# A static order planned with longer landings for two reciprocal rows and for queued transfers, with later second weights and fewer adding transfers

## The chip, the cores and the metric

The kernel runs on one core of a Trainium2 chip. Its engines run side by side, each through its own list of instructions: TensorE (PE; its weight loads are shown apart as PEld), VectorE (DVE), ScalarE (ACT), GpSimd (POOL) and SyncE (SP). ACT, POOL and SP also issue DMA transfers. The time is the device time of one execution in microseconds (us), the median of several runs.

## The reference

Four batches, 12 heads, 448 positions, head size 64; the model width is 768, the inner width 3072.

```python
scores = cap * tanh(scale * q @ k.T / cap)                 # soft cap
attn = exp(scores - max);  attn /= attn.sum(-1) + 1e-9
x = (attn @ v) laid out as [batch, seq, 768]
h = x.T @ U @ V                                            # U: 448x32, V: 32x448
u = x + h.T
out = u + relu(u @ w_ch1) @ w_ch2                          # 768 -> 3072 -> 768
```

## The kernel before

**The order.** The Python program lists some thousands of tasks. Each has its engine (or several to choose from) with a planned duration, what it reads and writes, a priority, and for a transfer a planned time to landing (`lat`) and a planned share of the DMA queues (`size`). `simulate` (from L155) plays the list once as a list scheduler: an engine that is free takes the ready task of the lowest priority number. `emit` then writes the tasks out in that order, engine by engine, with the semaphores that they need. So a planned number changes no instruction; it changes where the instructions stand. On the chip each engine keeps its order and waits where something comes later than planned. In `simulate` one clock, `moved`, stands for the DMA queues: each sized transfer pushes it on by its `size`, and the transfer counts as landed no earlier than `moved` + 500 ns.

**Attention** (to about 187 us) works on pairs of heads (p = 1 to 24). For two pairs at a time `normalize` (L591 to 632) makes the reciprocal of the softmax sums: PE sums by ones (L600), a copy, a small transfer that spreads the row over 32 partitions (L607), DVE's reciprocal (L616), a transfer to DRAM (L611, tile `rd`), two transfers that bring it back broadcast to 128 partitions (L624, tile `rb`), all three kinds issued by POOL; and DVE multiplies `u` by `rb` (L629, `norm`). `mixin` (from L634) then forms u = x + (x.T U V).T for the pair: PE transposes (L650) into two banks, two copies to `xx`, PE products with U (L666), a copy to `ys`, PE products with V (L677), and two additions on DVE (L684). The chains of the last two pairs (p of 20 and more) lie within the next stage.

**First layer, "up"** (L817; 185.5 to 509.6 us). u @ w_ch1 is formed by Strassen-Winograd with seven block products; each factor is split into a high and a low part, so that each task is nine matmuls of 128x128 by 128x448 into one PSUM bank `mm`. The batches 0 and 1 go first (n = 0, to about 350 us), then 2 and 3 (n = 1). In each there are 12 chunks of two weight blocks. A raw weight block comes as two words per value into one of two tiles `wr` (L739), is converted to `wa` (L328 on ACT, L333 and L336 on DVE), kept in DRAM (L749 for first weights, L746 for second weights, there `quad`), and made into the split operands `ws` by ACT and DVE (L717, L710). The results pass through `cx`: `keep` copies a bank to it on ACT (L272 from `up_seven`), DVE adds another bank to it (L830), and POOL stores it to DRAM as `mid` (L843). L272 is the copy helper that all stages use. The table `SECONDS` says how many blocks of w_ch2 are converted beside each chunk: entry 0 for n = 0, entry 1 for n = 1, entry 2 for the next stage.

**Second layer, "down"** (L963; 509.6 to 823 us). Three groups of inner blocks, in each the seven products of `PORDER`, each with six tasks of 12 matmuls. `weight` loads a weight quarter `wb` from `quad` (L889), `token` loads `gq` or `gw` from `mid` (L896); both are issued by SP. ACT and DVE split them into high and low parts (the weights into a tile that shows as `bw` or `wl`, the tokens into `g`; L272 and L908). Each finished bank is added to `u` by `onto`: on DVE (L983), or, every `EVERY`-th time, by an ACT copy to `st` (L272) and a POOL transfer that adds into `u` (L988). The last products of the last group send `u` out (L977).

Of the kernel before, what the change touches and what calls it, by code (L numbers as in the profile page):

```python
# [27 lines left out]
CF = 2  # L28
NCH = NF // CF
GROUPS = (0, 1), (2, 3), (4, 5)  # L30
EVERY = 3
SECONDS = (0, 0, 1, 0, 1, 0, 1, 0, 1, 0, 0, 0), (0, 0, 1, 1, 1, 1, 1, 2, 1, 2, 1, 1), (2, 2, 2, 2)
PORDER = 2, 1, 3, 6, 5, 7, 4


# [56 lines left out]
class Plan:  # L92
# [43 lines left out]
    def simulate(self):  # L136
# [11 lines left out]
        def rooms(bufs):  # L148
            taken, n, out = {}, {}, []
            for b in bufs:  # L150
                k = n.get(b.tag, 0)
                if self.order[b.tag][head[b.tag] + k] is not b:
                    return None
                n[b.tag] = k + 1
                for p in b.pools:  # L155
                    at = p, p.at(b)
                    if p.free[at[1]] > taken.get(at, 0) and all(not q.due for q in p.after):
                        taken[at] = taken.get(at, 0) + 1
                        out.append(p)
                        break  # L160
                else:
                    return None
            return out
# [14 lines left out]
        def start(t, e):  # L178
            new = [b for b in t.bufs if b.pool is None]
            for b, p in zip(new, rooms(new)):  # L180
                p.free[p.at(b)] -= 1
                b.pool = p
                b.slot = p.idle[p.at(b)].pop(0)
                head[b.tag] += 1
            cost = max(t.durs[e] - OVER.get(e, 0), 60) + (SWITCH if t.mode != mode[e] else 0)
            mode[e] = t.mode
            t.at, t.eng = now, e
            out.append(t)
            free[e] = now + cost
            if t.lock and e in locked:  # L190
                locked[e] = now + cost
            for o in t.durs:
                ready[o].remove(t)
            heapq.heappush(events, (now + cost, 1, t.i, "e"))
            done = now + cost + OVER.get(e, 0) + (LAT[e] if t.lat is None else t.lat)
            if t.size:
                self.moved = max(self.moved, now + cost + 1800) + t.size
                done = max(done, self.moved + 500)
            heapq.heappush(events, (done, 2, t.i, "d"))

        while True:
            for e in LAT:
                if free[e] <= now and ready[e]:
                    for t in sorted(ready[e], key=lambda t: (t.prio, t.i)):
                        if can(t, e):
                            start(t, e)
                            break
            if not events:
                break
            now = events[0][0]  # L210
            while events and events[0][0] == now:
                _, _, i, what = heapq.heappop(events)
                t = self.tasks[i]
# [65 lines left out]
class Build(Plan):  # L279
# [305 lines left out]
    def normalize(self, p):  # L585

        nc = self.nc
        prio = p - 100
        e = self.es[p - 1], self.es[p]
        rth, rj = self.rest[p]  # L590
        rest = p >= RESTS  # L591
        s = self.psum("misc")
        sr = self.buf("sr", [128, S], F32, self.an)
        r7 = self.buf("r7", [128, S // 32], F32, self.aq)
        u = self.u_bufs[p // NP]
        dram = {}

        def sums():
            for i in range(4):
                nc.tensor.matmul(  # L600
                    s.t[32 * i:32 * i + 32, :S], self.ones[:, 0], e[i % 2].t[:, i // 2], start=True, stop=not rest)
            for i in range(4 if rest else 0):
                nc.tensor.matmul(
                    s.t[32 * i:32 * i + 32, :S], self.ones[:, 1 + i % 2], rth.t[:, rj, i // 2], start=False, stop=True)

        def spread():
            nc.gpsimd.dma_start(out=r7.t, in_=sr.t[::32].rearrange("h (p f) -> h p f", p=32))  # L607

        def put():
            d = dram[0] = self.dp.tile([4, S], F32, tag="rd", name="rd", bufs=4)  # L610
            nc.gpsimd.dma_start(out=d.rearrange("a (p f) -> (a p) f", p=32), in_=r7.t)  # L611

        self.task({"PE": 1500 if rest else 750}, sums, r=[(e[0], 0), (e[1], 0), *([(rth, rj)] if rest else [])], w=[(s, 0)], prio=prio, mode="s")
        self.task({"DVE": 620, "ACT": 560}, lambda e: self.copy(e, sr.t, s.t[:, :S]), r=[(s, 0)], w=[(sr, 0)], prio=-300)
        self.task({"POOL": 700}, spread, r=[(sr, 0)], w=[(r7, 0)], lat=3000, prio=prio)
        self.task({"DVE": 250}, lambda: nc.vector.reciprocal(r7.t, r7.t), w=[(r7, 0)], prio=prio)  # L616
        self.task({"POOL": 600}, put, r=[(r7, 0)], w=[("rd", p)], lat=4000 if p < 20 else 2500, prio=prio)
        rb = self.buf("rb", [128, 2, S], F32, self.an)
        q = p % NP - 1

        def get():
            rows = dram[0].rearrange("(a i) s -> a (i s)", a=2)
            for a in range(2):
                nc.gpsimd.dma_start(  # L624
                    out=rb.t[64 * a:64 * a + 64].rearrange("p i s -> p (i s)"), in_=rows[a:a + 1].broadcast_to((64, 2 * S)))

        def norm():
            x = u.t[:, q:q + 2]
            nc.vector.tensor_tensor(out=x, in0=x, in1=rb.t, op=ALU.mult)  # L629

        self.task({"POOL": 1100}, get, r=[("rd", p)], w=[(rb, 0)], lat=7800 if p == 1 else 5000 if p < 20 else 3800, prio=prio)
        self.task({"DVE": 1090}, norm, r=[(rb, 0)], w=[(u, q), (u, q + 1)], prio=prio, lock=True)

    def mixin(self, b, pp):  # L634
# [139 lines left out]
    def moe(self):  # L774
# [4 lines left out]
        for n, bs in enumerate(((0, 1), (2, 3))):  # L779
            ws = None if n else self.strassen_weights(0, True, 60000, ALONE - 90, (self.wg,))  # L780
            xs = self.operands(bs, ORDER if n else EARLY, -50 if n else ALONE - 90)
            for c in range(NCH):
                prio = 3 if n or c < NCH - 2 else -60
                ws = ws or self.strassen_weights(c, n == 0, 0, prio)
                for _ in range(SECONDS[n][c]):
                    self.block(1, next(seconds), True, 0, 3)
# [94 lines left out]
    def down_all(self, order, seconds):  # L881


        nc, K, prio = self.nc, DM // 2, 3
# [26 lines left out]
        for ms in GROUPS:  # L911
            a, b, s2, w, g, bank = {}, {}, {}, {}, {}, {}
            last = ms is GROUPS[-1]
            for x, p in enumerate(PORDER):
                for _ in range(SECONDS[2][x - 3] if ms is GROUPS[0] and x > 2 else 0):
                    self.block(1, next(seconds), True, 0, prio, (self.cr,))
                for m in ms:
                    for i, j in {2: ((0, 1),), 1: ((0, 0),), 3: ((1, 0), (1, 1))}.get(p, ()):
# [13 lines left out]
                    x = w[p, m] = self.buf("wl", [128, 2, 2, K], F32R, self.bw, self.wq, self.cr)  # L932
# [18 lines left out]
                for n, bs in enumerate(((0, 1), (2, 3))):  # L951
                    u0, u1 = (self.u_bufs[i] for i in bs)
                    for d in range(3):
# [5 lines left out]
                        def products(p=p, n=n, d=d, ps=ps, fresh=fresh, w=w, g=g, ms=ms):  # L959
# [9 lines left out]
                            w=[(ps, 0)], prio=order, mode="mm")  # L969
# [3 lines left out]
                        for u, e in onto:  # L973
                            count += 1
                            self.onto(ps, lambda u=u, k=e: u.t[:, k], (u, e), count % EVERY == 0 and not (last and p in (7, 4)))
                            if last and p in (1, 5, 7, 4) and (p != 5 or e < 3):
# [69 lines left out]
```

## Time and profile before

| | |
|---|---|
| median of 3 runs | 829.42 us (828.74 to 830.03) |
| the profiled execution | 828.35 us; its span is 826.6 us, so 1.75 us lie outside the span |
| busy in the span | PE 805.9 us (97%), DVE 676.8 (82%), ACT 481.1 (58%), POOL 123.0 (15%) |
| mean granted TensorE clock | 0.993 of full speed |
| transfers | 164.28 MB, 199 GB/s on average |

The span is the time from the first to the last instruction of the profiled execution, and all stretches (such as 205.27) are counted from its start. A row of a timeline is a run of equal instructions of one engine: its start, its busy time, the engine, the line, the operation, output and input with one instruction's size, and in brackets how long the engine stood idle before it and what released it. The names of tiles stand without their numbers there. Matmuls overlap and their ends are modelled, so the distance from one start to the next is a better measure of a run than its busy time. The clock is given as a share of the full 2.4 GHz: 0.50 is the lower of the two levels, 1.2 GHz.

### The profile page before, as it was taken

The numbers are of one execution on the slowest core, as the hardware profiler recorded it, in microseconds if no ns is written. First come the engines' busy times: TensorE is split into PE (matmuls) and PEld (weight loads), VectorE is DVE, ScalarE is ACT, GpSimd is POOL, SyncE is SP. The second block draws the span as 40 slices with busy tenths as digits, with TensorE's granted clock in tenths as the row PEclk, the third lists the DMA queues.
The fourth block names the chain that finished last, engine by engine and source line by source line (L and its number), as shares of the span: only waits on it lengthen the run. The fifth ranks groups of instructions, "written<-read, shape, count | busy, mean of one in ns | idle before, by whom it ended". The sixth has DMA issues, their size and how long they took to land.

```text
span 826.6 us, 11913 instructions
## 1 busy us (share of the span) xinstructions
PE 805.9 (97%) x4344; PEld 639.0 (77%) x4344; DVE 676.8 (82%) x1067; ACT 481.1 (58%) x686; POOL 123.0 (15%) x193
## 2 busy tenths in 40 slices
PE   9999999997999999999999997999999999999998
PEld 4333333335899899989999996999999999999997
DVE  4778899988789888999786882899989987798653
ACT  7999999985565666565445543445444344433430
POOL 0111111111111111111111211011210112110110
PEclk9999999999899999999999999999999999999999
DMA  6453454526589897447866854977996477534252
GB/s 232 134 181 116 135 155 120 182 82 206 192 287 306 291 309 271 161 149 256 284 238 244 254 203 145 379 229 234 341 314 191 106 196 190 153 80 123 45 145 90
DMA packets 56109, 164.28 MB, mean 199 GB/s; under 512 B 7634, under 2 KB 22898, under 8 KB 56050
## 3 DMA queue, kind: packets, MB, share of 16 engines
q1 hardware_dynamic: 34736, 106.82, 39.4%
q0 software_dynamic: 14400, 37.82, 17.1%
q10 hardware_dynamic: 6914, 18.88, 5.8%
q8 instruction: 34, 0.56, 0.3%
q14 instruction: 25, 0.20, 0.1%
HBM read 106.81 MB, written 46.49 MB: 185 GB/s over the span
## 4 chain that ended last, share of the span: by engine, by line
PE 59%; DVE 2%; DMA 1%; issue 0%; ACT 0%; ACTq 0%
PE mm L963 37%; PE mm L817 22%; DMA wr<-in_w 1%; DVE cx L830 0%; DMA wb<-quad 0%; DVE x L717 0%; DVE wr L710 0%; ACT wa L328 0%; DVE ta L710 0%; DVE bw L908 0%; ACT bw L272 0%; DVE ws L717 0%; DVE u L983 0%; DVE wr L333 0%; DVE x L274 0%
## 5 line engine op out<-in xcount | busy, mean ns | idle before, releaser
L817 PE MATMUL mm<-x,ws 128*128 128x448 f32 x1404 | 291.3, 367 | 2.0 <-DVE cx L830 1.4
L817 PEld LDWEIGHTS mm<-x,ws 128*128 128x128 f32 x1404 | 263.6, 189 | 28.4 <-DVE cx L830 3.5
L963 PE MATMUL mm<-g,bw 128*128 128x448 f32 x756 | 176.1, 368 | 3.5 <-ACT bw L272 3.3
L963 PE MATMUL mm<-g,wl 128*128 128x448 f32 x756 | 174.0, 365 | 0.0
L963 PEld LDWEIGHTS mm<-g,bw 128*128 128x128 f32 x756 | 142.3, 188 | 16.2 <-ACT bw L272 3.6
L963 PEld LDWEIGHTS mm<-g,wl 128*128 128x128 f32 x756 | 142.6, 189 | 12.1 <-issue 0.2
L272 ACT ACTIVATE st<-mm 128x448 f32<-128x448 f32 x44 | 24.0, 546 | 142.4 <-issue 91.7
L843 POOL DMA_DIRECT2D mid<-cx x96 | 55.6, 580 | 258.2 <-ACT cx L272 252.7
L983 DVE TENSOR_TENSOR u<-u,mm 128x448 f32<-128x448 f32 x100 | 61.1, 616 | 36.6 <-PE mm L963 27.5
L272 ACT ACTIVATE cx<-mm 128x448 f32<-128x448 f32 x96 | 48.9, 543 | 61.7 <-PE mm L817 44.5
L503 PE MATMUL sc<-qk 64*128 64x448 f32 (+1 forms) x384 | 77.2, 569 | 0.3 <-ACT th L510 0.2
L521 ACT ACTIVATE th<-th,capt 128x1792 f32<-128x1792 f32 x42 | 76.1, 1811 | 0.6
L908 DVE TENSOR_TENSOR g<-gq,g 128x896 fp32r<-128x896 f32 x62 | 67.1, 1085 | 11.1 <-ACT g L272 10.1
L988 POOL DMA_DIRECT2D u<-st x44 | 38.3, 871 | 245.3 <-ACT st L272 229.1
L510 ACT ACTIVATE th<-sc 128x896 f32<-128x896 f32 x80 | 70.7, 940 | 5.4 <-PE sc L503 4.9
L272 ACT ACTIVATE g<-gq 128x896 fp32r<-128x896 f32 x62 | 57.6, 944 | 12.0 <-PE mm L963 9.8
L830 DVE TENSOR_TENSOR cx<-cx,mm 128x448 f32<-128x448 f32 x72 | 44.4, 616 | 20.9 <-PE mm L817 16.4
L567 DVE TENSOR_TENSOR es<-es,th 128x896 f32<-128x896 f32 (+1 forms) x48 | 51.9, 1081 | 11.5 <-ACT th L521 11.0
L272 ACT ACTIVATE cx<-cx 128x448 f32<-128x448 f32 x72 | 41.6, 577 | 31.4 <-DVE cx L830 30.7
L503 PEld LDWEIGHTS sc<-qk 64*128 64x128 f32 (+1 forms) x384 | 27.5, 175 | 40.1 <-issue 16.0
L561 PE MATMUL o<-th,vn 128*64 128x448 f32 x280 | 57.9, 548 | 0.0
L717 DVE TENSOR_TENSOR ws<-ta,ws 128x384 fp32r<-128x384 f32 x96 | 52.8, 552 | 2.5 <-ACT ws L272 1.5
(98 smaller groups left out, 828.2 us busy)
## 6 DMA issues: line engine op xcount, KB each, us to landing
wr<-in_w SPq DMA_DIRECT2D x48, 768.0 KB, 6.5
mid<-cx POOLq DMA_DIRECT2D x96, 224.0 KB, 4.3
gq<-mid SPq DMA_DIRECT2D x44, 448.0 KB, 5.7
qk<-in_qk SPq DMA_DIRECT2D x23, 448.0 KB, 4.0
u<-st POOLq DMA_DIRECT2D x44, 224.0 KB, 3.9
kept<-wa ACTq DMA_DIRECT2D x24, 384.0 KB, 6.5
quad<-wa ACTq DMA_DIRECT2D x24, 384.0 KB, 6.0
wb<-quad SPq DMA_DIRECT2D x24, 384.0 KB, 6.3
```

The source lines that it names most:

```text
L272: e.activation(out=out, in_=in_, func=func)
L503: nc.tensor.matmul(ps.t[out, a, :S], qks[c].t[hd, 1, 128 * t:min(S, 128 * t + 128)], qks[c].t[hd, 0], start=True, stop=True)
L510: nc.scalar.activation(out=th.t[:, j], in_=ps.t[:, :, :S], func=AF.Tanh, scale=(self.half if t == 3 else self.qsc) if raw else 1.0)
L521: nc.scalar.activation(out=th.t, in_=th.t, func=AF.Exp, scale=self.capt)
L561: nc.tensor.matmul(o.t[64 * a:64 * a + 64, :S], vn.t[:, 3 * i + t, a], th.t[:, j, a], start=False, stop=t == 2)
L567: e.tensor_tensor(out=out(), in0=in0(), in1=in1(), op=ALU.add)
L717: e.tensor_tensor(out=lo, in0=src(), in1=hi.bitcast(F32), op=ALU.subtract)
L817: nc.tensor.matmul(ps.t[:, :S], ws[p].t[:, wi, sl], xs[p].t[:, xi, d], start=fresh and n == 0, stop=n == 8, skip_group_check=not fresh)
L843: nc.gpsimd.dma_start(out=self.mid[at][:, c % 2], in_=to(x))
L908: self.task({"DVE": 130 + 1.09 * size}, lambda: nc.vector.tensor_tensor(out=lo(), in0=src.t, in1=hi().bitcast(F32), op=ALU.subtract), r=[( ...
L963: nc.tensor.matmul(ps.t[:, :S], w[p, m].t[:, wi, k, sl], g[p, n, m][gi].t[:, k], start=fresh and i == 0, stop=i == len(at) - 1, skip_group ...
L983: self.task({"DVE": 622}, lambda: nc.vector.tensor_tensor(out=out(), in0=out(), in1=ps.t[:, :S], op=ALU.add), r=[(ps, 0)], w=[key], prio=-200)
```

## The change

`EVERY` goes from 3 to 4: 33 in place of 44 evictions of the second layer are added by the POOL transfer, and 111 in place of 100 by DVE. Entry 2 of `SECONDS` is now read for the first two groups, product by product: the last eight second weight blocks are converted one at a time, from the fifth product of group 0 to the fifth of group 1, where they were converted two at a time from the fourth product of group 0 to its last. `simulate` counts 1.2 times the `size` of each transfer on the clock `moved`. And for the pairs of p = 20 and more the planned landing of `rd` is 5000 ns in place of 2500, and that of `rb` 9000 in place of 3800. But for the eleven evictions the kernel runs the same instructions on the same data.

```diff
-EVERY = 3
-SECONDS = (...), (...), (2, 2, 2, 2)
+EVERY = 4
+SECONDS = (...), (...), (0, 0, 0, 0, 1, 1, 1, 1, 1, 1, 1, 1, 0, 0)
...
             if t.size:
-                self.moved = max(self.moved, now + cost + 1800) + t.size
+                self.moved = max(self.moved, now + cost + 1800) + t.size * 1.2
...
-        self.task({"POOL": 600}, put, ..., lat=4000 if p < 20 else 2500, prio=prio)
+        self.task({"POOL": 600}, put, ..., lat=4000 if p < 20 else 5000, prio=prio)
...
-        self.task({"POOL": 1100}, get, ..., lat=7800 if p == 1 else 5000 if p < 20 else 3800, prio=prio)
+        self.task({"POOL": 1100}, get, ..., lat=7800 if p == 1 else 5000 if p < 20 else 9000, prio=prio)
...
             for x, p in enumerate(PORDER):
-                for _ in range(SECONDS[2][x - 3] if ms is GROUPS[0] and x > 2 else 0):
+                for _ in range(SECONDS[2][7 * GROUPS.index(ms) + x] if not last else 0):
                     self.block(1, next(seconds), True, 0, prio, (self.cr,))
```

The first place is PE's list behind the last attention products, where the mixing of the last two pairs (L650, L666, L677, twice) stands between products of the first layer. Before:

```order
L817 MATMUL mm<-x,ws 128x448 x18
L650 MATMUL misc<-ident,u_1412 112x64 x16
L817 MATMUL mm<-x,ws 128x448 x9
L666 MATMUL misc<-xx,ust 32x128 x8
L817 MATMUL mm<-bx,ws 128x448 x9
L677 MATMUL misc<-vst,ys 128x448 x2
L817 MATMUL mm<-x,ws 128x448 x9
L650 MATMUL misc<-ident,u_1412 112x64 x16
L817 MATMUL mm<-x,ws 128x448 x9
L666 MATMUL misc<-xx,ust 32x128 x8
L817 MATMUL mm<-x,ws 128x448 x9
L677 MATMUL misc<-vst,ys 128x448 x2
```

After, the same place (the list goes on with ten products in all, as before):

```order
L817 MATMUL mm<-x,ws 128x448 x27
L817 MATMUL mm<-bx,ws 128x448 x9
L817 MATMUL mm<-x,ws 128x448 x9
L650 MATMUL misc<-ident,u_1412 112x64 x16
L666 MATMUL misc<-xx,ust 32x128 x8
L677 MATMUL misc<-vst,ys 128x448 x2
L817 MATMUL mm<-x,ws 128x448 x27
L650 MATMUL misc<-ident,u_1412 112x64 x16
L817 MATMUL mm<-x,ws 128x448 x9
L666 MATMUL misc<-xx,ust 32x128 x8
L817 MATMUL mm<-x,ws 128x448 x9
L677 MATMUL misc<-vst,ys 128x448 x2
```

The first mixing now stands behind five products in place of two, with no product between its three steps; the second stands behind eight products in place of five.

The second place is POOL's list of the same time: the last pair's reciprocal row (`r7` to `rd` to `rb`) and the stores of the first layer's results (`mid`). Before:

```order
L607 DMA r7_1746<-sr_1735 128x1x14
L611 DMA rd_1810<-r7_1746 128x14
L624 DMA rb_1847<-rd_1810 64x896 x2
L843 DMA mid_1859<-cx_1824 128x448
L843 DMA mid_1932<-cx_1887 128x448
```

After:

```order
L607 DMA r7_1746<-sr_1735 128x1x14
L611 DMA rd_1789<-r7_1746 128x14
L843 DMA mid_1829<-cx_1793 128x448
L624 DMA rb_1854<-rd_1789 64x896 x2
L843 DMA mid_1909<-cx_1891 128x448
```

The first store of `mid` now stands ahead of the last pair's `rb`.

The third place is PE's list at the end of the first layer. The numbers tell tiles of one name apart; `mm` is the bank. Before:

```order
L817 MATMUL mm_4834<-x_3345,ws_4765 128x448 x9
L817 MATMUL mm_4806<-x_3370,ws_4784 128x448 x9
L817 MATMUL mm_4834<-x_3408,ws_4800 128x448 x9
L817 MATMUL mm_4834<-x_3448,ws_4816 128x448 x9
L963 MATMUL mm_4963<-g_3483,wl_3047 128x448
L963 MATMUL mm_4963<-g_3632,wl_3047 128x448
L963 MATMUL mm_4963<-g_3483,wl_3047 128x448 x2
L963 MATMUL mm_4963<-g_3632,wl_3047 128x448
L963 MATMUL mm_4963<-g_3483,wl_3047 128x448
L963 MATMUL mm_4963<-g_3643,bw_4948 128x448
```

After:

```order
L817 MATMUL mm_4790<-x_3371,ws_4787 128x448 x9
L817 MATMUL mm_4821<-x_3346,ws_4770 128x448 x9
L817 MATMUL mm_4821<-x_3419,ws_4802 128x448 x9
L817 MATMUL mm_4821<-x_3455,ws_4816 128x448 x9
L963 MATMUL mm_4913<-g_3501,bw_3479 128x448
L963 MATMUL mm_4913<-g_3680,bw_3479 128x448
L963 MATMUL mm_4913<-g_3501,bw_3479 128x448 x2
L963 MATMUL mm_4913<-g_3680,bw_3479 128x448
L963 MATMUL mm_4913<-g_3501,bw_3479 128x448
L963 MATMUL mm_4913<-g_3686,bw_3479 128x448
```

The last three products now use one bank, where before the last two did, and the second half of the first weights lies in another tile. Its load waits in SP's list for the room that a product's `ws` leaves: before that of the last product (ws_4816), now that of the fourth from the end (ws_4787).

## Rows read from the trace of the kernel before

**Rows 1.** Busy times of the engines in the span.

```profile
PE 805.9 (97%) x4344; PEld 639.0 (77%) x4344; DVE 676.8 (82%) x1067; ACT 481.1 (58%) x686; POOL 123.0 (15%) x193
```

**Rows 2.** What PE waited for: engine, line waited for, total, times, longest.

```profile
PE misc L650 <- DVE u L629: 4.6, 1, 4.6
...
PE mm L963 <- ACT bw L272: 3.3, 1, 3.3
...
PE misc L677 <- DVE ys L274: 1.0, 1, 1.0
```

**Rows 3.** Timeline of PE from the last attention products on.

```profile
188.43 3.98 PE L817 MATMUL mm<-x,ws 128*128 128x448 f32 x18
192.34 0.66 PE L650 MATMUL misc<-ident,u 64*112 64x64 f32 x16
...
198.63 2.09 PE L817 MATMUL mm<-x,ws 128*128 128x448 f32 x9
205.27 1.10 PE L650 MATMUL misc<-ident,u 64*112 64x64 f32 x16 [4.55 <-DVE u L629]
...
213.93 5.74 PE L817 MATMUL mm<-x,ws 128*128 128x448 f32 x27
219.51 2.02 PE L817 MATMUL mm<-bx,ws 128*128 128x448 f32 x9
```

**Rows 4.** Timeline of POOL there.

```profile
196.84 1.05 POOL L624 DMA_DIRECT2D rb<-rd  x2 [2.35 <-DMA rd<-r]
197.88 0.57 POOL L843 DMA_DIRECT2D mid<-cx  x1
```

**Rows 5.** Timeline of DVE there.

```profile
204.12 1.09 DVE L629 TENSOR_TENSOR u<-u,rb 128x896 f32<-128x896 f32 x1 [2.25 <-DMA rb<-rd]
```

**Rows 6.** Stretches: engines' busy us, granted clock (PEclk), DMA share, GB/s.

```profile
160.00:163.00 3.00, 1.49 (x12) 0.23 (x10) 2.35 (x3) 3.00 (x4) 0.71 (x1) 1.00 0.80 270
206.00:210.00 4.00, 4.00 (x21) 3.02 (x20) 2.09 (x5) 2.66 (x5) 0.55 (x1) 0.50 0.36 142
515.00:518.00 3.00, 2.81 (x8) 2.51 (x9) 1.09 (x2) 1.12 (x2) 0.00 (x0) 0.50 1.01 375
210.00:326.00 116.00, 115.39 (x575) 104.43 (x575) 99.86 (x186) 69.86 (x124) 20.43 (x35) 1.00 0.82 281
326.00:380.00 54.00, 53.29 (x262) 48.72 (x261) 53.64 (x112) 33.78 (x66) 9.40 (x16) 1.00 0.53 179
556.00:600.00 44.00, 44.00 (x218) 40.63 (x217) 43.61 (x56) 23.65 (x31) 6.87 (x8) 1.00 0.93 288
```

**Rows 7.** Timeline of PE across the end of the first layer.

```profile
507.62 2.08 PE L817 MATMUL mm<-x,ws 128*128 128x448 f32 x9 [0.71 <-DVE cx L830]
509.55 1.39 PE L963 MATMUL mm<-g,wl 128*128 128x448 f32 x6
514.20 0.72 PE L963 MATMUL mm<-g,bw 128*128 128x448 f32 x2 [3.26 <-ACT bw L272]
...
519.87 1.38 PE L963 MATMUL mm<-g,wl 128*128 128x448 f32 x6
...
522.30 0.96 PE L963 MATMUL mm<-g,wl 128*128 128x448 f32 x4
```

**Rows 8.** Timeline of SP's queue and DVE there.

```profile
509.74 1.84 SPq L889 DMA_DIRECT2D wb<-quad  x3
...
514.18 0.96 DVE L908 TENSOR_TENSOR bw<-wb,bw 128x768 fp32r<-128x768 f32 x1 [1.87 <-ACT bw L272]
```

**Rows 9.** Timeline of ACT between the mixing steps.

```profile
204.44 0.55 ACT L272 ACTIVATE cx<-mm 128x448 f32<-128x448 f32 x1 [4.33 <-DMA mid<-cx]
...
206.41 1.09 ACT L272 ACTIVATE xx<-misc 112x512 f32<-112x512 f32 x2
```

**Rows 10.** DVE's additions to u in the page: busy, mean ns | idle before.

```profile
L983 DVE TENSOR_TENSOR u<-u,mm 128x448 f32<-128x448 f32 x100 | 61.1, 616 | 36.6 <-PE mm L963 27.5
```

**Rows 11.** Loads of raw weights: count, KB each, median us to landing.

```profile
wr<-in_w SPq DMA_DIRECT2D x48, 768.0 KB, 6.5
```

More of the change, by code (lines that the diff above doesn't have):

```diff
@@ L30 @@
 GROUPS = (0, 1), (2, 3), (4, 5)
-EVERY = 3
-SECONDS = (0, 0, 1, 0, 1, 0, 1, 0, 1, 0, 0, 0), (0, 0, 1, 1, 1, 1, 1, 2, 1, 2, 1, 1), (2, 2, 2, 2)
+EVERY = 4
+SECONDS = (0, 0, 1, 0, 1, 0, 1, 0, 1, 0, 0, 0), (0, 0, 1, 1, 1, 1, 1, 2, 1, 2, 1, 1), (0, 0, 0, 0, 1, 1, 1, 1, 1, 1, 1, 1, 0, 0)
 PORDER = 2, 1, 3, 6, 5, 7, 4
@@ L616, in normalize @@
         self.task({"DVE": 250}, lambda: nc.vector.reciprocal(r7.t, r7.t), w=[(r7, 0)], prio=prio)
-        self.task({"POOL": 600}, put, r=[(r7, 0)], w=[("rd", p)], lat=4000 if p < 20 else 2500, prio=prio)
+        self.task({"POOL": 600}, put, r=[(r7, 0)], w=[("rd", p)], lat=4000 if p < 20 else 5000, prio=prio)
         rb = self.buf("rb", [128, 2, S], F32, self.an)
@@ L629, in norm @@
             nc.vector.tensor_tensor(out=x, in0=x, in1=rb.t, op=ALU.mult)
-        self.task({"POOL": 1100}, get, r=[("rd", p)], w=[(rb, 0)], lat=7800 if p == 1 else 5000 if p < 20 else 3800, prio=prio)
+        self.task({"POOL": 1100}, get, r=[("rd", p)], w=[(rb, 0)], lat=7800 if p == 1 else 5000 if p < 20 else 9000, prio=prio)
         self.task({"DVE": 1090}, norm, r=[(rb, 0)], w=[(u, q), (u, q + 1)], prio=prio, lock=True)
```

## The prediction

> **What bounds the kernel now.** I read the busy times first: PE works 805.9 of the 826.6 us span [rows 1], so only about 20 us of waits, and whatever its clock loses, can be won on PE without taking work away. The list of PE's waits then tells where: the two longest are one of 4.6 us ahead of a transpose (L650) that waits for DVE's `norm`, and one of 3.3 us ahead of the second layer's first weights [rows 2]. The change moves instructions at both places, so I read each in the timeline.
>
> Place one. PE starts the last pair's L650 at 205.27, after 4.55 us idle [rows 3]. `norm` started at 204.12, and DVE had waited for `rb` [rows 5], whose transfers POOL issued at 196.84 [rows 4]: 7.3 us from issue to use, where the plan counted 3.8 us. Then PE went on slowly: in 206 to 210 the granted clock was 0.50, the 1.2 GHz level [rows 6]. To price both together I compare two equal sequences (L650, a product, L666, a product, L677): 192.34 to 198.63 is 6.29 us, 205.27 to 213.93 is 8.66 us [rows 3]; the clock cost 2.37. A product takes 5.58 / 3 = 1.86 us (213.93 to 219.51), so the product at 198.63 ended at 200.49 and PE lost 205.27 - 200.49 = 4.78 by start times. Place one loses 2.37 + 4.78 = 7.15 us.
>
> Place two. From 519.87 to 522.30 twelve matmuls of the second layer take 2.43 us. The first 24 took from 509.55 to 519.87, 10.32 us, where 4.86 would do [rows 7]: a loss of 5.46, of which 3.26 is the wait and most of the rest the clock, again 0.50 in 515 to 518 [rows 6]. The cause is the load of the second half weight: SP issued it at 509.74, when the last product had freed its room, and the low half was ready at 514.18 + 0.96 = 515.14 [rows 8], 5.40 us after the issue.
>
> **The change part by part.** The profiled execution took 828.35 us, 1.07 less than the median 829.42; I take differences from the trace and subtract them from the median.
>
> *The longer landing times (5000 and 9000).* Ten products and two mixings stand in this stretch before and after; only their order changes. Now eight products and the whole first mixing stand ahead of the last L650. `rb` is issued later, because the first `mid` store stands ahead of it on POOL and waits for its `cx`; POOL issued that store right behind `rb` before, at 197.88 [rows 4], so I put `rb` 1 to 2 us later, at about 198.4. With the same 7.3 us it lands near 205.7 and `norm` (1.09) ends near 206.8. PE reaches the last L650 at 188.43 + 8 x 1.86 + one mixing (6.29 - 2 x 1.86 = 2.57) + the small waits below (2.9), near 208.8: some 2 us to spare, so the 4.78 goes. What is late next is small and new:
> - two products on one bank now follow each other directly. Such a pair cost 0.71 at 507.62 [rows 7]; I take 0.7.
> - the first mixing has no products between its steps. L666 must wait for the two `xx` copies, on ACT 1.09 us for both [rows 9], or half of that when DVE takes one, with hand-offs: 0.6 to 1.5, I take 1.2. L677 waits for `ys`: 0 to the 1.0 that one such wait cost [rows 2]; I take 0.5.
> - an ACT copy of a product's bank waited 4.33 us for a `mid` store to land [rows 9]. Before, PE's stall covered that; now the bank may be wanted sooner: 0 to 1.5, I take 0.5.
>
> These are 2.9 us. They are short and spread, so I count the clock loss as gone: 7.15 - 2.9 = 4.25, about 4.3 us won. The bounds: 7.15 if all of these hide, and 0.1 if the largest of each come together with the clock loss (7.15 - 0.7 - 1.5 - 1.0 - 1.5 - 2.37), which I do not expect.
>
> A rule speaks against leaving the clock out. In 160 to 163 PE was idle for half of the stretch (1.49 busy of 3.00) and the clock stayed at 1.00 [rows 6]; the clock fell here only after idle times of 4.55 and 3.26 us. The Trainium skill, page "TensorE: Matmul & The Clock Gate", section "A second HAM failure mode: psum-queue depth-cycling", says that frequent small idle times between groups of matmuls, as PE waits for PSUM, can also throttle the clock again. The new order makes just such small idle times; the row of 160 to 163 does not show that effect, and it gets a rival below.
>
> *The queue factor 1.2.* It makes the plan expect loads later. At place two the second half weight now takes the room of the fourth product from the end. Three products and two same-bank waits follow: 3 x 1.86 + 2 x 0.71 = 7.0 us before the second layer starts. The weight needs 5.40, so it is ready 1.6 us early and the wait and the slow clock go: 5.46. The last three products share one bank where two did, one more 0.71: 4.75 won, 4.7 for the sum. At the ends: 5.46 if that copy is hidden, and 0 if the load takes 5 us longer, in a queue as full as in 515 to 518 (share 1.01 [rows 6]).
>
> The factor also moves weight conversions of the first layer up to nine rows later in DVE's list. I cost that at nothing in 210 to 326, where DVE has 116 - 99.86 = 16.1 us free and PE idles 0.6 in all [rows 6]; without that cover it is the slower rival. In 326 to 380 DVE is busy 53.64 of 54 and PE idles 0.7 [rows 6]; nothing there hides a DVE delay.
>
> *EVERY.* 11 more additions on DVE at 616 ns, 6.8 us over the second layer; ACT loses 11 copies and POOL 11 transfers, both off the path. DVE spent 27.5 us there waiting for PE just ahead of such additions [rows 10], so the 6.8 fits, if not everywhere: in 556 to 600 DVE is busy 43.61 of 44 [rows 6]. There the next edit helps.
>
> *SECONDS.* Of the eight last blocks three, not eight, are converted in group 0. A block is two DVE passes (L333, L336) over 128x768, each about the 0.96 of a pass of that size [rows 8]: five blocks fewer are up to 9.6 us less for DVE in group 0, against about 2.2 us (3.5 additions in its 42 evictions) more. In group 1 they come back, beside fewer other loads; they are done by its fifth product, and the third group alone reads the last ones.
>
> In the second layer PE never waited before, but it now arrives 9 us earlier against a DVE that was full and queues at a share of 0.93 [rows 6]. I put 0.4 us for waits that may show, between 0 and 2.5.
>
> Sum: -4.3 - 4.7 + 0.4 = -8.6; 829.42 - 8.6 = 820.8 us. For the profiled execution this is 828.35 - 8.6 = 819.8.
>
> **The rivals.**
> A. DVE becomes the bound at the change from n = 0 to n = 1. For it: 53.64 of 54 us busy in 326 to 380. Against it: the 16.1 us free before, in which it can run ahead as far as tiles allow. PE would arrive 4.3 us earlier and wait 4.3 longer: 829.4 - 4.7 + 0.4 = 825.1.
> B. The second layer gives place two back. For it: DVE full and a DMA share of 0.93 in 556 to 600. Against it: no wait of PE anywhere in that layer before, and the lighter group 0. The 4.7 goes: 829.4 - 4.3 = 825.1, with a little more 825.5.
> C. The clock falls all the same, at one or both places, from several short waits. For it: the place has four of them within some 12 us. Against it: the row of 160 to 163. At 2.4 us each: 823.2 or 825.6. By the Trainium skill, the same page, section "Terms", the loss is the throttled time times one half; the rows above give 2.37 directly.
> D. Slower: the loads of raw weights are drawn out in n = 0. Two `wr` tiles hold the raw blocks, each load lands in 6.5 us [rows 11], and a tile is free only when its block is converted. If DVE reaches each conversion x later, each load starts x later, and with 20 of the 48 loads in 210 to 326, 20x adds up ahead of PE. Beyond x = 8.6 / 20 = 0.43 us, plus what the weights stand ahead of PE, the change is slower; at 0.55, 831.8. For it: conversions up to nine rows later, and a DMA share of 0.82. Against it: nine rows are a plan's order; DVE waits little, and if the block has not landed the row stands where it would have waited anyway.
> E. No change: `rb` lands still later than PE needs it (POOL's store ahead of it waits long), and the second half weight's load is issued as late as before because another SP entry ahead of it waits: 828 to 830.
>
> **How the numbers follow.** Forecast 0.60, with a range of its own of 817 to 824 (816.8 if stalls one and two are won whole, 7.15 and 5.46; 824 if 3 us of the small waits are added). A 0.12, B 0.08, C 0.07, D 0.08, E 0.05. The range 816 to 828 holds the forecast, A, B and C and leaves out D, most of E and the tails, under 0.2. About 0.2%, 1.7 us, is what a measurement can tell from no change. Faster: 0.60 + 0.12 + 0.08 + 0.07, less 0.01 for the tails, 0.86; the same: E and that 0.01, 0.06; slower: D, 0.08.
>
> **What would show it.** Right: PE's waits list has no entry above 1.5 us in 187 to 222, the stretch from the first of its products to the eleventh shrinks from 31.08 to some 26.8 us, and the clock there is 1.00; the second layer's first 24 matmuls take near 4.9 us, and the `wb` load is issued some 7 us before the first of them; the second layer lasts as long as before within 1 us. Wrong: an L650 wait for `norm` above 2 us, a clock of 0.50 at either place, new PE waits for `ws` operands in 210 to 380 (A, D), or for `g` or weights after 516 (B). D would show as longer gaps between loads of `wr`.

## The result and the profile after

The changed kernel took 821.88 us (median of 4 runs, 820.9 to 823.62) against 829.08 us before (4 runs): a ratio of 0.9917, 95% interval 0.9894 to 0.9941. It is 7.2 us faster; 820.8 us was forecast, with a range of 816 to 828. Run again later beside other kernels it took 820.9 us against 829.48 (0.9900, 0.9886 to 0.9915).

The span of the profiled execution is 820.5 us, that of the second profile 819.0. Cut at three starts of PE (the first of the ten products behind L600, the eleventh, the first L963), the spans divide so:

| us | before | changed | changed, second profile |
|---|---|---|---|
| up to the ten products | 188.43 | 191.68 | 189.20 |
| the ten products and two mixings (place one) | 31.08 | 27.21 | 27.23 |
| the rest of the first layer | 290.04 | 290.18 | 291.08 |
| second layer to the end (its start is place two) | 317.05 | 311.43 | 311.49 |

What PE waited for in the changed kernel (as in [rows 2]: engine, line waited for, total us, times, longest):

```profile
PE o L546 <- ACT th L521: 4.4, 4, 1.7
PE mm L817 <- ACT cx L272: 2.3, 4, 0.8
PE misc L677 <- DVE ys L274: 1.8, 1, 1.8
...
PE mm L817 <- DVE cx L830: 1.2, 2, 0.7
PE misc L666 <- DVE xx L274: 0.9, 1, 0.9
PE misc L650 <- DVE u L629: 0.4, 1, 0.4
PE misc L677 <- ACT ys L272: 0.4, 1, 0.4
```

The 4.6 us on L650 are 0.4, and no L963 is in the list. PE's timeline at place one answers to [rows 3]:

```profile
191.68 5.84 PE L817 MATMUL mm<-x,ws 128*128 128x448 f32 x27
198.15 2.09 PE L817 MATMUL mm<-bx,ws 128*128 128x448 f32 x9 [0.64 <-ACT cx L272]
200.08 1.98 PE L817 MATMUL mm<-x,ws 128*128 128x448 f32 x9
202.00 0.66 PE L650 MATMUL misc<-ident,u 64*112 64x64 f32 x16
203.56 0.64 PE L666 MATMUL misc<-xx,ust 112*32 112x128 f32 x16 [0.91 <-DVE xx L274]
204.59 1.02 PE L677 MATMUL misc<-vst,ys 64*128 64x448 f32 x4 [0.39 <-ACT ys L272]
206.39 5.71 PE L817 MATMUL mm<-x,ws 128*128 128x448 f32 x27 [0.77 <-ACT cx L272]
212.49 0.66 PE L650 MATMUL misc<-ident,u 64*112 64x64 f32 x16 [0.39 <-DVE u L629]
...
218.89 2.09 PE L817 MATMUL mm<-bx,ws 128*128 128x448 f32 x9
```

One long wait and a slow clock became five short waits, 0.64 + 0.91 + 0.39 + 0.77 + 0.39 = 3.10 us; each row's busy time is that of full speed (0.66 for L650, where [rows 3] has 1.10). The stretches of the changed kernel at both places have the full clock (columns as in [rows 6]):

```profile
185.00:210.00 25.00, 22.30 (x148) 15.97 (x141) 24.00 (x44) 13.82 (x27) 5.44 (x9) 1.00 0.54 180
...
510.00:516.00 6.00, 6.00 (x32) 5.54 (x31) 3.83 (x6) 3.23 (x4) 0.54 (x1) 1.00 0.85 286
```

POOL's and DVE's rows at place one, to be set beside [rows 4, 5]:

```profile
200.10 0.54 POOL L843 DMA_DIRECT2D mid<-cx  x1 [2.90 <-ACT cx L272]
201.31 1.49 POOL L624 DMA_DIRECT2D rb<-rd  x2 [0.67 <-DVE u L629]
```

```profile
211.34 1.08 DVE L629 TENSOR_TENSOR u<-u,rb 128x896 f32<-128x896 f32 x1
```

`rb` is issued behind the store of `mid`, and then waits for the first pair's `norm`, which reads the same tile.

Place two, PE's timeline (as [rows 7]):

```profile
504.35 2.08 PE L817 MATMUL mm<-x,ws 128*128 128x448 f32 x9 [0.68 <-ACT cx L272]
507.14 2.08 PE L817 MATMUL mm<-x,ws 128*128 128x448 f32 x9 [0.71 <-DVE cx L830]
509.07 6.27 PE L963 MATMUL mm<-g,bw 128*128 128x448 f32 x30
```

and the timeline of all engines (as [rows 8]):

```profile
501.89 8.59 SPq L889 DMA_DIRECT2D wb<-quad  x3
...
505.48 0.85 ACT L272 ACTIVATE bw<-wb 128x768 fp32r<-128x768 f32 x1
...
507.00 0.95 DVE L908 TENSOR_TENSOR bw<-wb,bw 128x768 fp32r<-128x768 f32 x1
```

The load goes out 7.2 us ahead of the first L963, and its low half is ready at 507.95, 1.1 us ahead. The first 30 matmuls of the second layer take 6.27 us; before, the first 24 took 10.32.

The first row of the table is no part of the change: the instruction lists of all engines are the same there in both kernels. In the first profile PE waited 1.84 us for `ys` at 78.17; the twelve L503 behind it took 3.17 us busy, where those of before took 1.83. PE's timeline of the changed kernel:

```profile
78.17 1.02 PE L677 MATMUL misc<-vst,ys 64*128 64x448 f32 x4 [1.84 <-DVE ys L274]
79.02 3.17 PE L503 MATMUL sc<-qk 64*128 64x448 f32 x12
```

and of the kernel before:

```profile
76.76 1.02 PE L677 MATMUL misc<-vst,ys 64*128 64x448 f32 x4 [0.96 <-DVE ys L274]
77.62 1.83 PE L503 MATMUL sc<-qk 64*128 64x448 f32 x12
```

### The profile page after: what moved, and what is told of

The parts are those of the page before. It is cut to its first block, busy times and chain, and to the rows that moved or that the text cites. A ratio compares the mean times of both kernels' runs of the same rounds, so it can differ in the third digit from the quotient of the medians.

```text
span 820.5 us, 11851 instructions
## 1 busy us (share of the span) xinstructions
PE 803.5 (98%) x4344; PEld 636.9 (78%) x4344; DVE 684.6 (83%) x1083; ACT 473.6 (58%) x670; POOL 111.4 (14%) x182
## 4 chain that ended last, share of the span: by engine, by line
PE 84%; DVE 8%; DMA 4%; ACT 2%; issue 2%; POOL 0%; ACTq 0%; DVEq 0%; POOLq 0%
PE mm L963 37%; PE mm L817 35%; PE sc L503 4%; PE o L561 3%; DVE es L567 3%; DMA rd<-r 1%; DMA rb<-rd 1%; DMA quad<-wa 1%; PE o L546 1%; DVE x L717 1%; PE misc L424 1%; ACT th L521 1%; ACT th L510 1%; DVE u L629 1%; DVE wr L710 1%
## 5 line engine op out<-in xcount | busy, mean ns | idle before, releaser
L963 PE MATMUL mm<-g,bw 128*128 128x448 f32 x756 | 169.4, 366 | 0.0
L963 PE MATMUL mm<-g,wl 128*128 128x448 f32 x756 | 168.0, 365 | 0.0
L963 PEld LDWEIGHTS mm<-g,bw 128*128 128x128 f32 x756 | 142.0, 188 | 11.8
L963 PEld LDWEIGHTS mm<-g,wl 128*128 128x128 f32 x756 | 142.0, 188 | 11.8
L983 DVE TENSOR_TENSOR u<-u,mm 128x448 f32<-128x448 f32 x111 | 67.5, 616 | 42.2 <-PE mm L963 39.2
L843 POOL DMA_DIRECT2D mid<-cx x96 | 53.3, 555 | 258.6 <-ACT cx L272 250.1
L503 PE MATMUL sc<-qk 64*128 64x448 f32 (+1 forms) x384 | 79.0, 584 | 0.3 <-ACT th L510 0.3
L272 ACT ACTIVATE st<-mm 128x448 f32<-128x448 f32 x33 | 18.0, 544 | 78.0 <-PE mm L963 44.7
L988 POOL DMA_DIRECT2D u<-st x33 | 28.6, 868 | 249.4 <-ACT st L272 240.6
L503 PEld LDWEIGHTS sc<-qk 64*128 64x128 f32 (+1 forms) x384 | 27.7, 178 | 41.1 <-issue 16.8
L328 ACT ACTIVATE wa<-wr 128x768 f32<-128x768 f32 (+2 forms) x50 | 44.4, 889 | 18.5 <-DMA quad<-wa 6.5
```

Source lines behind the costliest of these rows:

```text
L272: e.activation(out=out, in_=in_, func=func)
L328: nc.scalar.activation(out=a_t(), in_=raw_t()[:, 1::2].bitcast(F32), func=AF.Prelu, scale=2.0 ** -112, alpha=-(2.0 ** 32))
L503: nc.tensor.matmul(ps.t[out, a, :S], qks[c].t[hd, 1, 128 * t:min(S, 128 * t + 128)], qks[c].t[hd, 0], start=True, stop=True)
L843: nc.gpsimd.dma_start(out=self.mid[at][:, c % 2], in_=to(x))
L963: nc.tensor.matmul(ps.t[:, :S], w[p, m].t[:, wi, k, sl], g[p, n, m][gi].t[:, k], start=fresh and i == 0, stop=i == len(at) - 1, skip_group ...
L983: self.task({"DVE": 622}, lambda: nc.vector.tensor_tensor(out=out(), in0=out(), in1=ps.t[:, :S], op=ALU.add), r=[(ps, 0)], w=[key], prio=-200)
```

## The experiments

Times are medians with their runs beside those of the kernel before on the same chip; the ratio has its 95% interval. The kernel before took 828.08 to 829.48 us there. "lat" stands for the two landing times.

| kernel | us | ratio to before |
|---|---|---|
| only lat | 819.7 | 0.9887 (0.9871 to 0.9904) |
| only the queue factor | 826.64 | 0.9968 (0.9958 to 0.9979) |
| only EVERY and SECONDS | 829.52 | 1.0004 (0.9991 to 1.0016) |
| all (the changed kernel again) | 820.9 | 0.9900 (0.9886 to 0.9915) |
| before, one weight load earlier | 824.16 | 0.9939 (0.9927 to 0.9951) |
| lat, EVERY, SECONDS | 818.73 | 0.9883 (0.9869 to 0.9897) |
| only lat, 12000 for rb | 827.09 | 0.9968 (0.9953 to 0.9983) |
| factor, EVERY, SECONDS | 824.13 | 0.9943 (0.9931 to 0.9956) |
| factor, SECONDS | 825.35 | 0.9971 (0.9960 to 0.9982) |
| EVERY, SECONDS, lat 2500 and 5500 | 819.66 | 0.9877 (0.9860 to 0.9894) |
| EVERY, SECONDS, lat 2500 and 9000 | 818.74 | 0.9870 (0.9847 to 0.9893) |
| EVERY, SECONDS, lat 6000 and 9000 | 821.1 | 0.9899 (0.9884 to 0.9914) |

**Only the landing times.**

```diff
-... lat=4000 if p < 20 else 2500, prio=prio)
+... lat=4000 if p < 20 else 5000, prio=prio)
-... 5000 if p < 20 else 3800, prio=prio)
+... 5000 if p < 20 else 9000, prio=prio)
```

> Only the two longer landing times (5000 and 9000). The prediction gave them place one alone: PE's 4.6 us wait for norm and the slow clock behind it go, the stretch of ten products takes 27.2 us as in the changed kernel (31.1 before), the second layer's start is as slow as before; about 825 us against 829 of before. The rival theory: the numbers move everything that the plan lists behind them, and in this kernel's SP list the load of the second half of the first down weights stands six entries earlier than before; then place two is cured too (no 3.3 us wait there, its 24 first matmuls near 4.9 us) and the time is 820 to 822, all that the whole change brought.

Measured 819.7, 0.3 under the rival's range; the theory's 825 fell. The two numbers cure place one and place two. PE's timeline at the end of the first layer:

```profile
493.83 8.47 PE L817 MATMUL mm<-x,ws 128*128 128x448 f32 x41
502.14 1.38 PE L963 MATMUL mm<-g,wl 128*128 128x448 f32 x6
503.36 1.39 PE L963 MATMUL mm<-g,bw 128*128 128x448 f32 x6
504.58 2.00 PE L817 MATMUL mm<-x,ws 128*128 128x448 f32 x9
```

and the load of the second half weight in SP's queue:

```profile
467.74 0.53 SPq L889 DMA_DIRECT2D wb<-quad  x1
```

It goes out 34 us ahead of the first L963, where the changed kernel has 7.2. The second layer starts without a wait; and since its first task now stands ahead of the last product of the first layer, the two waits of one bank (0.68 and 0.71 in the changed kernel) are hidden too.

**Only the queue factor.**

```diff
-self.moved = max(self.moved, now + cost + 1800) + t.size
+self.moved = max(self.moved, now + cost + 1800) + t.size * 1.2
```

> Only the queue factor 1.2. The prediction gave it place two alone: the wait of 4.6 us for norm stays with its slow clock, the start of the second layer takes 4.9 us in place of 10.3; about 824 to 825 us. The rival theory (place two is cured by any new plan, and the factor also delays weights): the same place two, but waits of PE for split weights in the first layer, 827 us or more.

Measured 826.64, between the theory (824 to 825) and the rival (827 or more). PE's waits:

```profile
PE misc L650 <- DVE u L629: 4.4, 1, 4.4
...
PE mm L963 <- ACT g L272: 1.0, 1, 1.0
PE mm L963 <- DVE g L908: 0.9, 1, 0.9
```

Place one stays, place two is cured, but the second layer now waits at 540 us. No wait for `ws` appears, so the rival's mechanism did not come either. ACT's timeline shows what held `g` back:

```profile
537.85 0.55 ACT L272 ACTIVATE st<-mm 128x448 f32<-128x448 f32 x1 [3.79 <-PE mm L963]
538.29 0.84 ACT L272 ACTIVATE wl<-wt 128x768 fp32r<-128x768 f32 x1
539.02 0.94 ACT L272 ACTIVATE g<-gq 128x896 fp32r<-128x896 f32 x1
```

ACT stood idle for 3.79 us at the copy `st` of an adding transfer, which needs a bank that PE finishes late; the copies of `wl` and `g` that PE wants next are queued behind it.

**Only EVERY and SECONDS** (the two edits of the diff, with the loop's index).

> Only EVERY = 4 and the later second weights. The lists of PE up to the second layer are those of before, so both places stay as they were. The prediction: PE never waited in the second layer and does not now, so within 1 us of before (828 to 830). The rival: fewer adding transfers and spread weight loads free the queues or DVE, so that the second layer gets shorter by over 1 us, or the 11 more additions on DVE make PE wait there and the time is over 830.

Measured no change, as the prediction had it. Both places were as before (5.2 us on L650, 3.3 on L963).

**The changed kernel again** (no edit).

> The changed kernel once more. In its first profile a product of V waited 1.84 us at 76 us, the clock was low from about 79 to 82.5 us, and all that followed came 3 us later, though the instruction lists up to there are those of before (in the profile of before the wait there was 0.96 us and the clock stayed). If that is a chance of the single execution, some profiles of these runs show it and some not, whichever kernel, and this one without it would take about 819.5; if it belongs to the changed kernel, this profile shows it again and the kernels that share its beginning differ from it.

Measured 820.9; the second profile has a wait of 1.21 us for `ys` and a mean clock of 1.000 (0.998 in the first profile). The lists up to there are those of before and the second profile does not have it, so the low clock near 80 us does not come from the change; in the profiles of the other kernels the same wait was 0.84 to 1.50 us. What made it 1.84 in one execution is not known.

**One weight load earlier, nothing else.**

```diff
-... size=1250, prio=prio)
+... size=1250, prio=2 if (m, i, j) == (1, 0, 1) else prio)
```

> The kernel before with one edit: the load of the first down weights' second half has priority 2 in the plan. Its SP entry moves ten places up; the lists of all engines up to about 450 us are those of before, so place one stays as it is (wait of 4.6 us, slow clock). It tells the price of place two by itself. The theory: the wait of 3.3 us, the slow clock behind it (5.5 us together) and one wait of 0.7 us of two products on one bank go, 823.3 to 824.2 us. The rival: the second layer gives part of it back, as the kernel with the queue factor alone did (two waits for g at 540 us), 826 or more.

Measured 824.16, 5.0 us less than before. The load stood at 452.90 in SP's timeline, and no wait was left at the start of the second layer. L650 still waited 5.0 us at place one. Two waits for `g` of 0.6 and 0.3 us after 570 give a little back. Place two is worth 5 us by itself, and the forecast's 4.7 is of that size.

**The changed kernel without the factor.**

```diff
-self.moved = max(self.moved, now + cost + 1800) + t.size * 1.2
+self.moved = max(self.moved, now + cost + 1800) + t.size
```

> The changed kernel without the queue factor 1.2. The landing times alone gave 819.7, EVERY and SECONDS alone nothing. The theory: the factor brings nothing once the landing times are longer, and costs the 1.4 us of two waits of products on one bank at the end of the first layer; without it 819 to 820. The rival: EVERY and SECONDS cost something here, or the factor is what made the difference; 821 or more.

Measured 818.73, a little under the expected 819 to 820. The waits of 0.68 and 0.71 us at the end of the first layer are not in its timeline. The intervals of this kernel and the changed one overlap, so that the factor costs something is likely and not shown.

**The landing time of rb at 12000.**

```diff
-... 5000 if p < 20 else 3800, prio=prio)
+... 5000 if p < 20 else 12000, prio=prio)
```

(with 5000 for rd)

> Only the landing times, with 12000 for rb in place of 9000. Each step of the two mixings has a product between, and ten products stand ahead of the last transposes where eight did. The theory: the waits for xx, ys and norm at place one (0.9, 0.4 and 0.8 in the kernel with 9000) go, some 1.5 to 2 us; 818. The rival: place one's waits were covered by something else that now comes last (DVE's or ACT's queue), or the later mixing delays the operands of n = 1; 819.5 or more.

Measured 827.09: the rival, and more than it said. PE's timeline:

```profile
201.01 0.66 PE L650 MATMUL misc<-ident,u 64*112 64x64 f32 x16 [1.62 <-DVE u L629]
203.35 3.73 PE L817 MATMUL mm<-x,ws 128*128 128x448 f32 x9 [1.68 <-ACT cx L272]
207.01 1.08 PE L666 MATMUL misc<-xx,ust 112*32 112x128 f32 x16
```

and the stretch behind them (columns as in [rows 6]):

```profile
203.00:206.00 3.00, 2.65 (x7) 2.39 (x8) 2.42 (x6) 1.98 (x4) 0.57 (x1) 0.50 0.82 272
```

The first pair's `norm` was put so late that L650 waited for it, a copy of a bank to `cx` came late as well, and behind these two waits the clock was 0.50. PE's waits for ACT's `cx` are 6.0 us in sum (2.3 in the changed kernel).

**The changed kernel without lat, and the factor with SECONDS alone** (EVERY = 3).

> The changed kernel without the longer landing times. The queue factor alone gave 826.6: place two was cured, but PE waited 1.0 and 0.9 us for g at 540 us and its clock fell there. The theory: the later second weights and fewer adding transfers take conversions off DVE and ACT in group 0, so that those waits go; place one stays; 823.5 to 825. The rival: the waits at 540 us come from the tokens' loads, which those edits don't reach; they stay, 826 to 827.

> The queue factor and the later second weights, EVERY left at 3. The factor alone gave 826.6 with two waits for g at 540 us and a low clock behind them; with EVERY and SECONDS 824.1. The theory: SECONDS did that, since the conversion of a raw block stood on DVE at 533.6 and 535.9, just ahead of the late g, and is gone there; 823.5 to 824.7, with no wait over 0.7 us after 516. The rival: EVERY did it, by fewer ACT copies and adding transfers; the waits stay, 826 to 827.

Measured 824.13 and 825.35. With EVERY = 4 the two waits at 540 us were gone (PE waited 0.3 us at 542 and 0.6 at 546 instead); with SECONDS alone they stood as before, 1.04 and 0.91, so the theory that SECONDS removes them fell and the rival's mechanism holds, though 825.35 lies between the two ranges. The intervals of these two, 0.9931 to 0.9956 and 0.9960 to 0.9982, do not overlap. ACT's rows show why: with EVERY = 4 no copy `st` stands ahead of the `g` in question. No run moved that copy alone. ACT's timeline of the kernel with EVERY = 4:

```profile
536.76 0.94 ACT L272 ACTIVATE g<-gq 128x896 fp32r<-128x896 f32 x1
540.11 0.55 ACT L272 ACTIVATE st<-mm 128x448 f32<-128x448 f32 x1 [2.42 <-PE mm L963]
```

**Other landing times, with EVERY and SECONDS and no factor.** The numbers for rd and rb are 2500 and 5500, 2500 and 9000, 6000 and 9000.

> EVERY and SECONDS as changed, no queue factor, landing times of 2500 and 5500 for rd and rb (changed: 5000 and 9000; with those and no factor 818.7). The first mixing now stands behind three products, with one product between its steps, and the store of mid still ahead of the last pair's rb. The theory: place one's limit is when the last pair's norm can run, and that starts with the first pair's norm, since the second rb transfer waits until the first norm has read the tile; an earlier first mixing hides the xx and ys waits and the same-bank wait (1.9 us in sum) and does not move the last norm later; 817 to 818.5. The rival: PE gets to the last transposes earlier than the norm, waits over 1.5 us more, and the clock falls; 820 or more.

> The same with 2500 and 9000: only the planned landing of rb is longer, that of rd as before the change. In POOL's list the last pair's rb now stands ahead of the mid store, as before the change; the first mixing stands behind four products and the last transposes behind eight. The theory: longer planned landing for rb alone is enough for places one and two, 817.5 to 819.5, since PE's list gives eight products of cover in any case. The rival: both numbers are needed, L650 waits over 2 us again, 821 or more.

> The same with 6000 and 9000: the last transposes stand behind nine products in place of eight. The theory: the 0.7 us that L650 still waited for norm go, and nothing else changes at place one; 818.0 (818.7 without this). The rival, from the kernel with 12000: later mixing makes ACT's copies of banks wait (they were 6.0 us in all there) and the time goes up; 820 or more.

Measured 819.66, 818.74 and 821.1. The first misses its theory: L650 did not wait, but PE waited 2.84 us for a copy to `cx`, and that copy for the landing of a store. ACT's timeline:

```profile
203.63 0.54 ACT L272 ACTIVATE cx<-mm 128x448 f32<-128x448 f32 x1 [3.94 <-DMA mid<-cx]
```

This is the same wait as in [rows 9], where PE's stall had covered it. The second meets its theory: with EVERY and SECONDS, which give nothing by themselves, a longer landing of `rb` alone is enough. The third meets its rival: L650 no longer waits, but a copy to `cx` makes PE wait 1.90 us at 211 us.

In the first and the third the granted clock fell behind that wait, and rose again some 3 us later. The kernel with 2500 and 5500:

```profile
204.40:207.60 3.20, 3.20 (x9) 2.85 (x10) 1.93 (x4) 1.05 (x2) 0.57 (x1) 0.50 0.99 339
```

and the one with 6000 and 9000:

```profile
211.60:214.40 2.80, 2.80 (x8) 2.50 (x9) 0.32 (x1) 1.20 (x2) 0.54 (x1) 0.50 0.88 361
```

The lowest medians are 818.73 (the changed kernel without the factor) and 818.74; both lie under the kernel before beyond the intervals, and under the changed kernel by the median only: its second interval, 0.9886 to 0.9915, overlaps theirs.

## Why the prediction was right, and where it was not

**Place one** was forecast at 4.3 us and measured at 31.08 - 27.21 = 3.87 (3.85 in the second profile). The terms left over were put at 2.9 us and are 3.10: the bank 0.64 (0.7 forecast), `xx` 0.91 (1.2), `ys` 0.39 (0.5), the ACT copy 0.77 (0.5), and 0.39 for `norm`, put at nothing. The ACT copy came late for another reason than the forecast's: not a `mid` store's landing but a copy of `ws` ahead of it in ACT's list, which waited 0.84 us for DVE. `rb` was issued 201.31 - 191.68 = 9.63 us into the stretch, 8.41 before: 1.2 us later, as forecast (1 to 2). Only half of the reason was seen: besides the store, the first pair's `norm` holds `rb` back. `norm` started 19.66 us into the stretch where I put it at 17.3. The two transfers of `rb` had landed 4.7 to 5.2 us after their issue (6.3 to 6.7 before), by 207.0, and DVE had no idle time ahead of `norm` at 211.34, so DVE's own list, not the landing, set it. Of the 2 us to spare that the prediction counted nothing was left: L650 waited 0.39.

**Place two** was forecast at 4.7 and measured, in the table, at 317.05 - 311.43 = 5.62, of which one more wait of a shared bank (0.68) is given back in the first layer: 4.9. The early load alone gave 5.0.

**The second layer's give-back** of 0.4 did not show: 311.43 is 0.16 under the 317.05 - 5.46 = 311.59 of place two cured. Rival B's loss did happen in the kernel with the factor alone, through ACT's list and not through a full DVE or the queues. **Rivals A, D and E** did not come: the rest of the first layer takes 290.18 and, in the second profile, 291.08 where it took 290.04, with the extra bank's 0.68 in it (A would add 4.3); L650 and the load are both early enough, against E.

**The wrong step** is the division between the edits. The prediction gave place two to the queue factor. The runs show that the landing times alone cure it too: in all six kernels with longer landing times and no factor that load goes out 34 us ahead of the first L963, and no wait is left there. With them the factor is not needed, and in the changed kernel, which has both, the load goes out only 7.2 us ahead. Cut by edits, the gain is the landing times' (9.8 us alone), the factor's is 2.8 alone, and it is not a sum.

**EVERY and SECONDS** were priced at nothing, and by themselves that holds. With the factor and without the landing times, EVERY = 4 is worth 0.9971 against 0.9943, some 2.3 us. In the single profiles of these two the time from the first L963 to the end is 314.58 us with EVERY = 4 and 315.85 with 3 (317.27 with the factor alone, where the clock fell at 541 us). The step that failed there is that the saved copies on ACT are off the path: a copy that waits for PE in ACT's list holds back those that PE needs next. The changed kernel has `st` copies like it, and no wait of PE behind one. A reading behind SECONDS was also off: of a block's two passes on DVE, put at 0.96 each, L333 takes 0.56 on average, so five blocks are some 7.5 us and not 9.6; no wait turned on it.

**Rival C**, the clock, did not come in the changed kernel: the rows of place one run at full speed with five waits of up to 0.91 us. That does not show the effect of frequent small idle times that the Trainium skill's page "TensorE: Matmul & The Clock Gate", section "A second HAM failure mode: psum-queue depth-cycling", describes. In three of the other orders the clock did fall to 0.50 at place one: behind 1.62 and 1.68 us (12000), behind 2.84 us (2500 and 5500) and behind 1.90 us (6000 and 9000), and in each a wait for a PSUM bank was among them. These are one or two waits and not frequent ones, so whether they are the page's effect is not shown. That the clock was left out of the sum held for this order and not for those three.

**The total** is in part luck. The 1.1 us between the first median (821.88) and the forecast may come from the low clock near 80 us: up to the ten products the first profile is 191.68 - 189.20 = 2.48 us longer than the second, and the first four runs of the changed kernel have a mean clock of 0.998 to 0.999, the later four 0.999 to 1.000. That all of the first four had it is not shown. The second median (820.9) meets the forecast to 0.1 us, but in its profile the two places give 3.85 + 5.56 = 9.41 us, and 0.77 and 1.04 us are lost again before and between them.

## What to carry to other kernels

Where a planner sets a static order, a wrong duration can cost twice, as here: at the wait itself and in the order of what is planned later. So an edit's worth is found by undoing it alone and by doing it alone, not by adding terms. A cover of products ahead of a late landing pays until its own producers (here `norm` and the copies to `cx`) are moved late by it: 9000 gained, 12000 lost most of it. An instruction that waits for the engine it serves must not stand ahead of copies that this engine needs next.

## What the runs showed of the hardware

The clock does not follow one wait's length alone. Behind 1.04 and 0.91 us of idle time at 540 us the granted clock was 0.50 in one kernel's profile and 1.00 in another's, with the same rows of waits. The kernel with the factor alone:

```profile
541.40:544.00 2.60, 2.60 (x7) 2.34 (x8) 2.60 (x3) 0.97 (x2) 0.00 (x0) 0.50 1.04 415
```

and the one with the factor and SECONDS:

```profile
541.40:544.00 2.60, 2.59 (x13) 2.42 (x14) 2.60 (x3) 0.99 (x2) 0.00 (x0) 1.00 1.02 409
```

Single waits of 1.69 us (ending at 165.51, changed kernel) and 1.65 us (at 211 us, the kernel with 2500 and 9000) left it at 1.00. 1.84 us (ending at 78.17, changed kernel) was followed by 0.54, and the 1.90 and 2.84 us of the kernels with 6000 and 9000 and with 2500 and 5500 by 0.50 (their rows stand above). The changed kernel's rows:

```profile
79.00:82.00 3.00, 3.00 (x14) 0.49 (x10) 3.00 (x6) 1.25 (x2) 0.00 (x0) 0.54 0.24 69
165.50:168.00 2.50, 2.49 (x30) 1.33 (x32) 2.33 (x4) 2.47 (x3) 0.00 (x0) 1.00 0.85 303
```

What decides it stays open; no run here varied the waits alone.
